# Splitting each attention layer's last unit into two head pairs, with a PSUM bank reserved for the first pair's prologue

## The chip, the cores and the metric

The kernel runs on one core of a Trainium2 chip. The metric is the device time of one execution, in microseconds (us). "Clock" is the mean granted clock of TensorE, as a share of full speed, as the profile's windows give it. PE is TensorE, ACT is ScalarE, DVE is VectorE, POOL is GpSimd. All times are of fast runs, unless a run is called slow.

## The reference, cut to what matters

```python
def _A_ref(x, wq, wk, wv, wo):            # S = 2048, D = 512, 32 heads of 16, one k and one v for all heads
    q = ((x @ wq).reshape(B, S, H, Dh)).transpose(0, 2, 1, 3)
    k = x @ wk;  v = x @ wv
    scores = einsum("bhqd,bkd->bhqk", q, k) * (Dh ** -0.5)
    o = einsum("bhqk,bkd->bhqd", softmax(scores), v)
    return o.transpose(0, 2, 1, 3).reshape(B, S, H * Dh) @ wo
def _B_ref(x, w_gate, w_up, w_down):      # hidden size 1792
    return (gelu(x @ w_gate) * (x @ w_up)) @ w_down
x = A_x                                   # then the same two blocks, twice
x = x + _A_ref(_layernorm(x), ...);  x = x + _B_ref(_layernorm(x), ...)
x = x + _A_ref(_layernorm(x), ...);  x = x + _B_ref(_layernorm(x), ...)
```

## The kernel before

Each attention layer is cut into 32 units of 512 queries and four heads. A unit goes through two passes and a step between them:

- Pass 1 computes scores with the queries on the partitions, and DVE takes the row maxima: 32 pairs of score matmuls, 32 reductions.
- The prologue turns the maxima into extra rows of the query operand, so that the second pass's matmul subtracts them by itself: a combine on DVE, three small POOL steps, four PE transposes into a PSUM bank, a copy by ACT (named AUGS in the profile), and two small DMAs.
- Pass 2 computes the scores again, with the keys on the partitions: 64 matmuls, 64 exponentials on ACT, and 16 groups of four matmuls with V ("PV"), which use four column tiles of the PE array.

The kernel has a static list scheduler of its own. The program is written unit by unit: the query projection of unit u+2, pass 1 and prologue of unit u, the epilogue (normalization, and at times the output projection) of unit u-1, pass 2 of unit u. So pass 1 of a unit runs beside pass 2 of the unit before. PSUM banks 0 to 3 belong to pass 1, bank 7 to PV, and banks 4 to 6 are handed round by `take_c` to everything else. Who waits for a bank is fixed by the order in which the program takes it.

```python
C_B = [4, 5, 6]
PV_B = 7
def take_c():
    b = C_B[cnt["nC"] % 3]
    cnt["nC"] += 1
    return b

def pass1_and_prologue(u):
    for pair in range(NBLK // 2):                       # 32
        ...
        mm = P.add("pe", ... matmul(PS[:, b, :], lhsT=QA[...], rhs=KA[a][...]) ...)      # mm1, L728
        rd = P.add("dve", ... tensor_reduce(out=PM[...], in_=PS[:, b0:b0 + 2, :], ...))  # L734
    cmb = P.add("dve", ...)                             # combine, L746
    hi = P.add("pool", ...); ng = P.add("pool", ...); lo = P.add("pool", ...)
    M_B = take_c()
    ...                                                 # 4 transposes into M_B, L768
    aev = P.add("act", ... out=AUGS[0:8, slot, :], in_=PSB[M_B][0:8, 0:512] ...)         # L771
    for k in range(2):
        dmas.append(P.add("sp", ... dma_start(QA[16 + k:16 + k + 97:32, ...], AUGS[...]) ...))   # L777

def pass2(u):
    for kb in range(NKB):                               # 16 key blocks
        for jj in range(4):
            ...
            b = take_c()
            deps = banks.deps(b)
            if kb == 0 and jj == 0:
                deps = deps + dmas                      # the unit's first score waits for the prologue
            mm = P.add("pe", ... matmul(PS[:, b, :], lhsT=KA[a][...], rhs=QA[...]) ...)  # mm2, L799
            ex = P.add("act", ... activation(out=PT[:, buf, :], in_=PS[:, b, :], func=ACTF.Exp, scale=SCALE) ...)  # L810
            banks.release(b, [ex])
        for j in range(4):
            pv = P.add("pe", ... matmul(PS[32 * j:32 * j + 32, PV_B, :], lhsT=VA[:, kb, :], rhs=PT[:, buf, :],
                       tile_position=(0, 32 * j)), ..., grp=(4 if j == 0 else 1), ...)   # L824

for u in range(NU + 1):
    if u < NU:
        if u + QAHEAD < NU:
            q_proj(u + QAHEAD)
        pass1_and_prologue(u)
    if u >= 1:
        epilogue(u - 1)
    if u < NU:
        pass2(u)
```

`grp` is the number of matmuls that the scheduler keeps together on PE. The rest of this text calls the pass 2 of a layer's last unit, unit 31, the layer's tail.

## Time and profile before

The kernel took 2896.9 us, the median of four runs (2896.36 to 2900.84).

| What (profile of before) | Value |
|---|---|
| Share of the chain that ended last: row maxima on DVE / exponentials on ACT | 58% / 17% |
| A steady unit: 32 reductions | 36.5 us |
| 64 exponentials beside them | 31.46 us |
| Tail of layer 1: 64 exponentials | 37.76 us (1249.50 to 1287.26) |
| Last exponential of unit 30 to first of unit 31 | 4.97 us |
| Granted clock in the tail | 0.50 |

The first lines are of the profile page of before: the busy times, the clock in tenths over 40 slices of the span, the chain that ended last by line, and the two costliest groups (line, engine, operation, destination and source, count, then busy time, mean ns of one, idle time before them and what ended most of it).

```profile
PE 2553.5 (88%) x15853; PEld 925.4 (32%) x15968; DVE 2545.3 (88%) x2650; ACT 2336.6 (81%) x4720; POOL 167.0 (6%) x375
...
PEclk8799999999999999969969999999999999999699
...
DVE PM L734 58%; ACT SH L810 17%; PE PS L970 3%; PE PS L963 3%; PE PS L992 3%; PE PS L799 3%; PE PS L728 1%; PE PS L824 1%; ACT XNT L583 1%; PE PS L904 1%; PE PS L665 1%; PE PS L574 1%; DMA QA<-AUGS 1%; ACT ONT L892 1%; PE PS L621 0%
...
L734 DVE TENSOR_REDUCE PM<-PS 128x2 f32<-128x1024 f32 x2048 | 2329.4, 1211 | 22.4 <-PE PS L728 15.3
L810 ACT ACTIVATE SH<-PS 128x512 bf16<-128x512 f32 x4096 | 2019.5, 692 | 114.2 <-PE PS L799 114.1
```

DVE's row maxima bound the steady units, and the change takes none of them away. What it can alter is where the tail has no partner. The clock line dips to 6 tenths in three of the 40 slices; the 18th (1231 to 1303 us) and the 38th (2678 to 2751 us) hold the two tails.

The next lines are of the timeline of ACT around the first layer's end, in before. Columns: start us, us, engine, line, operation, count, and in brackets the idle time before it and what ended it.

```profile
1213.07 31.46 ACT L810 ACTIVATE SH<-PS 128x512 bf16<-128x512 f32 x64 [2.12 <-PE PS L799]
...
1246.21 0.57 ACT L771 ACTIVATE AUGS<-PS 8x512 bf16<-8x512 bf16 x1
...
1249.50 3.53 ACT L810 ACTIVATE SH<-PS 128x512 bf16<-128x512 f32 x7 [2.24 <-PE PS L799]
1253.34 2.06 ACT L810 ACTIVATE SH<-PS 128x512 bf16<-128x512 f32 x4 [0.31 <-PE PS L799]
...
1286.66 0.60 ACT L810 ACTIVATE SH<-PS 128x512 bf16<-128x512 f32 x1 [0.32 <-PE PS L799]
1287.28 1.28 ACT L976 ACT_TABLE_LOAD   x1
```

Unit 30's 64 exponentials run without a break. Then ACT waits for the prologue of unit 31, and from 1253 on it stops 0.32 us after every four exponentials: ACT is no longer what limits the tail, PE is. The windows of before show why. Columns: window, its length, busy us and instructions of PE, PE's weight loads, DVE, ACT and POOL, then the clock, the DMA share and GB/s.

```profile
1243.82:1247.24 3.42, 2.75 (x28) 1.98 (x28) 2.57 (x7) 3.33 (x7) 0.97 (x3) 1.00 0.00 0
1247.24:1250.65 3.41, 1.20 (x7) 0.24 (x5) 0.63 (x3) 1.17 (x4) 1.57 (x3) 1.00 0.01 2
1250.65:1254.06 3.41, 3.15 (x11) 0.67 (x11) 0.00 (x0) 3.10 (x7) 0.00 (x0) 0.50 0.00 0
1256.00:1264.00 8.00, 6.95 (x26) 1.35 (x25) 0.00 (x0) 7.05 (x15) 0.00 (x0) 0.50 0.00 0
```

At half clock a score matmul takes 0.60 us and a PV group 0.62 us, and the chain of four exponentials is 2.38 us, against 1.97 us for four exponentials at ACT's own pace. One turn of this chain, from before's PE timeline:

```profile
1261.14 0.60 PE L799 MATMUL PS<-QA,KA 64*128 64x512 bf16 x1 [0.26 <-ACT SH L810]
1261.67 0.62 PE L824 MATMUL PS<-SH,VA 128*32 128x512 bf16 x4
1262.22 1.03 PE L799 MATMUL PS<-QA,KA 64*128 64x512 bf16 x3
```

### The profile page before, as it was taken

To read this page: it belongs to the slowest core of one execution; us is meant where nothing else is said; L and a number is where in the kernel's file an instruction comes from. 1 tells how busy PE (TensorE), PEld (TensorE's weight loads), DVE (VectorE), ACT (ScalarE), POOL (GpSimd) and SP (SyncE) were. 2 spreads that over 40 slices of the span, in tenths; PEclk is the share of its full clock that TensorE was granted. 3 is DMA by queue.
4 is the path that set the end of the run, shared out by engine and by line. 5 is a ranking of instruction groups with operands and counts; after the bars stand their busy time and mean duration, and the time that the engine had idled before them with its cause. 6 is when DMAs were issued, how large, how long until landed. Compare 5 with 4: busy or idle time off the path is not lost.

```text
span 2895.3 us, 40074 instructions
## 1 busy us (share of the span) xinstructions
PE 2553.5 (88%) x15853; PEld 925.4 (32%) x15968; DVE 2545.3 (88%) x2650; ACT 2336.6 (81%) x4720; POOL 167.0 (6%) x375
## 2 busy tenths in 40 slices
PE   4899999899999899889968999888999999888898
PEld 1222232222222222227722222222232223222366
DVE  6999999999999999925569999999999999999143
ACT  2699989998999899973418999899989999999632
POOL 3000000001000100010000000100010001000100
PEclk8799999999999999969969999999999999999699
DMA  3000000000000000000000000000000000000000
GB/s 120 1 1 1 1 1 1 1 1 1 1 1 1 1 1 1 1 1 1 1 1 1 1 1 1 1 1 1 1 1 1 1 1 1 1 1 1 1 16 16
DMA packets 10413, 13.88 MB, mean 5 GB/s; under 512 B 1776, under 2 KB 9200, under 8 KB 10224
## 3 DMA queue, kind: packets, MB, share of 16 engines
q1 hardware_dynamic: 10224, 11.31, 1.2%
q8 instruction: 125, 2.05, 0.3%
q14 instruction: 64, 0.52, 0.1%
HBM read 8.68 MB, written 2.10 MB: 4 GB/s over the span
## 4 chain that ended last, share of the span: by engine, by line
DVE 60%; ACT 20%; PE 18%; issue 1%; DMA 1%; POOL 1%; SPq 0%; DVEq 0%; ACTq 0%
DVE PM L734 58%; ACT SH L810 17%; PE PS L970 3%; PE PS L963 3%; PE PS L992 3%; PE PS L799 3%; PE PS L728 1%; PE PS L824 1%; ACT XNT L583 1%; PE PS L904 1%; PE PS L665 1%; PE PS L574 1%; DMA QA<-AUGS 1%; ACT ONT L892 1%; PE PS L621 0%
## 5 line engine op out<-in xcount | busy, mean ns | idle before, releaser
L734 DVE TENSOR_REDUCE PM<-PS 128x2 f32<-128x1024 f32 x2048 | 2329.4, 1211 | 22.4 <-PE PS L728 15.3
L810 ACT ACTIVATE SH<-PS 128x512 bf16<-128x512 f32 x4096 | 2019.5, 692 | 114.2 <-PE PS L799 114.1
L799 PE MATMUL PS<-QA,KA 64*128 64x512 bf16 x4096 | 1470.9, 399 | 119.6 <-ACT SH L810 17.0
L728 PE MATMUL PS<-KA,QA 64*128 64x512 bf16 x4096 | 1003.0, 398 | 125.5 <-DVE PM L734 117.9
L799 PEld LDWEIGHTS PS<-QA,KA 64*128 64x128 bf16 x4096 | 370.6, 94 | 1059.2 <-ACT SH L810 1000.9
L824 PE MATMUL PS<-SH,VA 128*32 128x512 bf16 x4096 | 425.5, 401 | 0.3
L728 PEld LDWEIGHTS PS<-KA,QA 64*128 64x128 bf16 x4096 | 203.8, 94 | 387.3 <-DVE PM L734 306.1
L981 DVE TENSOR_TENSOR HT<-PS,GEL 128x256 bf16<-128x256 f32 x224 | 94.8, 423 | 257.2 <-PE PS L970 166.3
L976 ACT ACTIVATE GEL<-PS 128x256 bf16<-128x256 f32 x224 | 85.9, 384 | 192.1 <-PE PS L963 192.1
L824 PEld LDWEIGHTS PS<-SH,VA 128*32 128x32 bf16 x4096 | 107.6, 93 | 247.4 <-issue 245.8
L970 PE MATMUL PS<-XNT,WU 128*128 128x256 bf16 x896 | 134.5, 273 | 2.3 <-ACT XNT L583 2.3
L963 PE MATMUL PS<-XNT,WG 128*128 128x256 bf16 x896 | 134.4, 273 | 0.0
L754 POOL TENSOR_SCALAR MHL<-MXC 128x16 bf16<-128x16 f32 x64 | 16.3, 255 | 1962.9 <-DVE MXC L746 1962.9
L992 PE MATMUL PS<-WD,HT 128*128 128x512 bf16 x403 | 123.7, 379 | 5.3 <-DVE HT L981 2.4
L771 ACT ACTIVATE AUGS<-PS 8x512 bf16<-8x512 bf16 x64 | 37.2, 581 | 85.6 <-PE PS L768 84.8
L963 PEld LDWEIGHTS PS<-XNT,WG 128*128 128x128 bf16 x896 | 86.9, 98 | 51.9 <-ACT RT L911 0.6
L970 PEld LDWEIGHTS PS<-XNT,WU 128*128 128x128 bf16 x896 | 86.9, 98 | 14.8 <-ACT XNT L583 4.8
L672 ACT ACTIVATE QA<-PS 128x512 bf16<-128x512 f32 x60 | 35.8, 597 | 44.1 <-PE PS L665 44.1
L665 PE MATMUL PS<-XNT,WQP 128*128 128x512 bf16 x196 | 55.5, 400 | 10.6 <-ACT SH L810 8.2
L574 PE MATMUL PS<-IDENT_B,XN 128*128 128x128 bf16 x256 | 28.5, 247 | 39.6 <-ACT XNT L583 20.6
L583 ACT ACTIVATE XNT<-PS 128x512 bf16<-128x512 bf16 x64 | 37.3, 595 | 30.2 <-PE PS L574 30.0
L869 POOL TENSOR_TENSOR SH<-OT,RI 128x256 bf16<-128x256 f32 x64 | 39.7, 620 | 362.0 <-DVE RI L862 357.3
(67 smaller groups left out, 673.7 us busy)
## 6 DMA issues: line engine op xcount, KB each, us to landing
SH<-in_A_x_dram SPq DMA_DIRECT2D x4, 512.0 KB
QA<-AUGS SPq DMA_DIRECT2D x128, 4.0 KB
out_dram<-SH SPq DMA_DIRECT2D x4, 512.0 KB, 2.9
WG<-in_B_w_gate_dram SPq DMA_DIRECT2D x1, 1792.0 KB
WU<-in_B_w_up_dram SPq DMA_DIRECT2D x1, 1792.0 KB
WD<-in_B_w_down_dram SPq DMA_DIRECT2D x1, 1792.0 KB
ONT<-in_A_wq_dram SPq DMA_DIRECT2D x1, 512.0 KB
WO<-in_A_wo_dram SPq DMA_DIRECT2D x1, 512.0 KB
```

What stands on the lines that cost most here:

```text
L583: ev = P.add("act", lambda e, tb=tb, b=b: e.activation(out=XNT[:, :, tb * 128:(tb + 1) * 128], in_=PSB[b][:, 0:NCC * 128].rearrange("p (c ...
L665: mm = P.add("pe", lambda e, cc=cc, qc=qc, g=g, b=b: e.matmul(PS[:, b, :], lhsT=WQP[:, cc, g, :], rhs=XNT[:, cc, qc * 512:(qc + 1) * 512], ...
L728: mm = P.add("pe", lambda e, b=b, tt=tt, a=a, g=g, qc=qc, qb=qb, kc=kc: e.matmul(PS[:, b, :], lhsT=QA[64 * tt:64 * tt + 64, g, (4 * qc + q ...
L734: rd = P.add("dve", lambda e, b0=b0, slot=slot, c0=c0: e.tensor_reduce(out=PM[:, slot, c0:c0 + 2 * NKC + 1:2 * NKC], in_=PS[:, b0:b0 + 2, ...
L799: mm = P.add("pe", lambda e, b=b, tt=tt, a=a, g=g, qc=qc, kb=kb: e.matmul(PS[:, b, :], lhsT=KA[a][64 * tt:64 * tt + 64, kb * 128:(kb + 1) ...
L810: ex = P.add("act", lambda e, b=b, buf=buf: e.activation(out=PT[:, buf, :], in_=PS[:, b, :], func=ACTF.Exp, scale=SCALE), [mm] + bdeps + x ...
L824: pv = P.add("pe", lambda e, j=j, kb=kb, buf=bufs[j]: e.matmul(PS[32 * j:32 * j + 32, PV_B, :], lhsT=VA[:, kb, :], rhs=PT[:, buf, :], star ...
L963: mg = P.add("pe", lambda e, cc=cc, fc=fc, t0=t0, G_B=G_B: e.matmul(PS[:, G_B, 0:256], lhsT=WG[:, cc, fc * 128:(fc + 1) * 128], rhs=XNT[:, ...
L970: mu = P.add("pe", lambda e, cc=cc, fc=fc, t0=t0, U_B=U_B: e.matmul(PS[:, U_B, 0:256], lhsT=WU[:, cc, fc * 128:(fc + 1) * 128], rhs=XNT[:, ...
L976: ga = P.add("act", lambda e, gs=gs, G_B=G_B: e.activation(out=GEL[:, gs, 0:256], in_=PS[:, G_B, 0:256], func=ACTF.Gelu_apprx_tanh), [mg] ...
L981: hm = P.add("dve", lambda e, gs=gs, hs=hs, U_B=U_B: e.tensor_tensor(out=HT[:, hs, 0:256], in0=PS[:, U_B, 0:256], in1=GEL[:, gs, 0:256], o ...
L992: dmm[qb] = P.add("pe", lambda e, pfc=pfc, phs=phs, qb=qb: e.matmul(PS[:, D_B[qb], 0:D], lhsT=HT[:, phs, qb * 128:(qb + 1) * 128], rhs=WD[ ...
```

## The change

The intent is to hide the last unit's prologue. The last unit of each layer becomes two half units, head pair 0 and head pair 1. Each half has its own query copy (QAX, so the prologue's DMA into one half does not touch the other), 16 reductions, 32 exponentials, and PV groups of two. The first half's prologue can then run while unit 30's exponentials are still going, and the second half's while the first half's are. A prologue there needs a PSUM bank in the middle of a pass 2 that was written before it, so the bank is reserved at that point of pass 2 (after 30 of unit 30's 64 scores; after 26 of the first half's 32), and later users of it wait for the prologue's copy.

```diff
+    def reserve(self, b):
+        res = dict(bank=b, before=list(self.rel[b]), waiters=[], done=False)
+        self.rel[b] = []
+        self.pending[b] = res
+        return res
+    def note_user(self, b, op): ...          # the next user of a reserved bank is put on its waiters
+    def fulfill(self, res, release_op):      # ... and waits for the prologue's copy
+        for w in res["waiters"]:
+            w.deps.append(release_op)
 ...
+        QAX = sb("QAX", [128, max(1, 2 * NSPLIT), 512], BF16)      # NSPLIT = 1
 ...
+            for u in range(NU):
+                if u >= NU - NSPLIT:
+                    subs.append((u, [0], False))
+                    subs.append((u, [1], True))
+                else:
+                    subs.append((u, [0, 1], True))
 ...
-                M_B = take_c()
+                res = st.get("reserved")
+                if res is not None:
+                    M_B = res["bank"]
+                    bdeps = res["before"]
+                else:
+                    M_B = take_c()
 ...
-            def pass2(u):
+            def pass2(si, reserve_at=None):
 ...
+                            if reserve_at is not None and nblk == reserve_at:
+                                st["reserved"] = banks.reserve(take_c())
 ...
-                            deps, est=214, q=Q_PV, lane=("col", j), grp=(4 if j == 0 else 1), name="pv", banks=[PV_B])
+                            deps, est=214, q=Q_PV, lane=("col", j), grp=(nh if idx == 0 else 1), name="pv", banks=[PV_B])
 ...
+                        nb = 2 * len(subs[si][1]) * NKB
+                        r_at = max(0, nb // 2 - 2) if len(subs[si][1]) == 2 else max(0, nb - 6)
+                    pass2(si, reserve_at=r_at)
```

## The prediction

> **What bounds the kernel now.** The chain of waits gives 58% of the span to DVE's row-maximum reductions (2048, about 1.13 us apart), 17% to ACT's exponentials. In each of two attention layers 32 units are pipelined: unit u's 32 reductions (36.5 us on DVE) run beside unit u-1's 64 exponentials (31.46 us, 0.49 each). There DVE is full, and the change alters no work. What it can alter is each layer's end, where the last unit's exponentials have no partner. Timeline of layer 1: last reduction ends 1244.15; the prologue (combine, three POOL steps, transposes, copy, DMA) until the first exponential at 1249.50; exponentials until 1287.26: 37.8 us for 64, not 31.46. Layer 2 is the same.
>
> **Why this tail is slow.** In the windows table the granted clock is 1.00 up to 1250.65, then 0.50 until 1298.4. In slices of 3.41 us (the grid of this trace's clock changes), the one before the fall (1247.24 to 1250.65) has PE busy only 1.20 us: PE waits 1.6 us for the prologue's DMA. [...] At half clock the tail's chain is score matmul 0.60, PV 0.55, score matmul 0.59, exponential 0.59 = 2.38 us per four exponentials, against 1.97 at ACT's own rate.
>
> **What the change does.** The last unit becomes two halves (16 reductions, 32 exponentials each). The first half's prologue runs amid unit 30's exponentials, in a bank reserved there; the second's amid the first half's exponentials (after 26 of 32, by the built order). It adds one ACT copy (0.6 us, in ACT's slack), a second small prologue, and twice as many PV groups, of two. It does not overlap more reductions with exponentials: all 32 still run beside unit 30. The gain is only
>
> 1. the 5.0 us between unit 30's last exponential (1244.5) and the next (1249.5), of which four ACT evacuations (2 us) plus about 0.8 us of waits remain: -2.2 us;
> 2. no DMA wait on PE, so I expect the clock to stay at 1.00 and the tail to run at ACT's rate: 31.5 instead of 37.8 us: -6.3 us;
> 3. costs: AUGS copy and reserved bank's stall in unit 30's exponentials, +1.0 to +1.5 us; second AUGS copy +0.5 us.
>
> Net about -6.5 us per layer, all on the critical path: -13 us. The epilogue after the tail (13 us) has its own PE gaps; I give it no gain.
>
> **Predicted: 2884 us, 8-in-10 range 2873 to 2896.** Faster by over 2%: 0.01; within 2%: 0.98; slower by over 2%: 0.01.
>
> **What would show it.** Timeline of ACT: no gap over 1 us between the last reduction and the following exponentials; last exponential some 36 us after unit 30's last, not 42.7; gaps of 0.32 us per four exponentials gone. Windows: clock 1.00 through most of the tail. Score matmul in the tail 0.39, not 0.60 us. Around unit 30's 32nd exponential one ACT gap near 1 us with the AUGS copy. Steady units unchanged.
>
> **What would make it wrong.** If a lull at the handover still drops the clock, PV groups of two alternate with score pairs at half clock (about 1.2 us per two exponentials, or worse) and step 2 is lost: 2890 to 2900. If the reserved bank stalls PE long enough to starve DVE, step 3 grows. If the epilogue also keeps full clock, 3 us more per layer.

Its sum is -2.2 - 6.3 + 1.5 to + 2.0 us, about -6.5 us per layer and -13 us in all. That the clock would stay at 1.00 (step 2) was the estimate from before's windows (PE busy for 1.20 of 3.41 us before the fall).

## The result, and the profile after

The changed kernel took 2885.6 us (median of 9 runs, 2883.59 to 2895.17); before took 2896.56 us in the same rounds (13 runs, 2894.91 to 2902.26). The ratio is 0.9964, with a 95% interval of 0.9955 to 0.9974: within 2%. Ratios here are the mean time of one kernel's fast runs over that of the other's fast runs of the same rounds, so not quite the ratio of the medians quoted. 0.9964 of 2896.9 us is a gain of 10.4 us.

The same lines of the page of after (line 793 is the reductions, 906 the exponentials, 894 the second pass's scores, 920 PV):

```profile
PE 2552.2 (89%) x15861; PEld 928.0 (32%) x15976; DVE 2546.4 (88%) x2652; ACT 2335.2 (81%) x4724; POOL 167.8 (6%) x382
...
PEclk8799999999999999999968999999999999999999
```

The work is the same within a few us on every engine; what differs is the clock: the dips of the 18th and the 38th slice are gone. The timeline of ACT around the first layer's end, in after:

```profile
1210.57 3.72 ACT L906 ACTIVATE SH<-PS 128x512 bf16<-128x512 f32 x7 [2.12 <-PE PS L894]
...
1227.37 0.57 ACT L851 ACTIVATE AUGS<-PS 8x512 bf16<-8x512 bf16 x1
1228.42 15.79 ACT L906 ACTIVATE SH<-PS 128x512 bf16<-128x512 f32 x32 [0.48 <-PE PS L894]
...
1249.25 11.87 ACT L906 ACTIVATE SH<-PS 128x512 bf16<-128x512 f32 x24 [1.77 <-PE PS L894]
1260.82 0.59 ACT L851 ACTIVATE AUGS<-PS 8x512 bf16<-8x512 bf16 x1
1261.31 2.96 ACT L906 ACTIVATE SH<-PS 128x512 bf16<-128x512 f32 x6
1264.48 15.79 ACT L906 ACTIVATE SH<-PS 128x512 bf16<-128x512 f32 x32 [0.22 <-PE PS L894]
1280.29 1.28 ACT L1078 ACT_TABLE_LOAD   x1
```

The first half's AUGS copy now stands in the middle of unit 30's exponentials, where it and the wait for the reserved bank cost 1.05 us (0.57 + 0.48). The second stands in the first half's exponentials and costs 0.5 us. After 1249.25 the exponentials run at ACT's pace, 0.49 us each, in runs of 24 and 32 without the stops of 0.32 us. The windows of after (same columns as above):

```profile
1240.00:1244.00 4.00, 3.58 (x23) 1.10 (x21) 3.31 (x5) 4.00 (x9) 0.65 (x3) 1.00 0.00 0
1244.00:1248.00 4.00, 3.61 (x20) 1.78 (x20) 2.48 (x7) 3.25 (x7) 0.22 (x1) 0.63 0.00 0
1256.00:1264.00 8.00, 7.69 (x35) 2.29 (x35) 0.00 (x0) 8.00 (x18) 0.00 (x0) 1.00 0.01 2
```

In layer 1 the clock falls at the handover and comes back within one window of 3.41 us. In layer 2 it does not fall there at all. In both layers it also falls for two windows at the start of unit 30 (1210.90 to 1217.73 us in layer 1), where before's clock stayed at 1.00.

The following table is worked out from the timelines of ACT, for both layers; it is the yardstick for the experiments too. "Last two units" is from the first exponential of unit 30 to the end of the last of unit 31. "Epilogue" is from there until the FFN's steady stream of GELUs begins. At ACT's pace, the exponentials of "last two units" would take 2 x 31.46 = 62.9 us; the rest is waiting, copies, and PE at half clock.

| Kernel (profiled run) | Last two units, layer 1 / 2 | Epilogue, layer 1 / 2 |
|---|---|---|
| before | 74.19 / 74.19 | 13.54 / 13.48 |
| after | 69.70 / 68.19 | 14.20 / 13.07 |

The gain in these segments is 4.49 + 6.00 - 0.66 + 0.41 = 10.2 us, which is the gain that the runs show. The two profiled runs differ by more (2895.3 and 2882.5 us); 2.5 us of that are in layer 1 before unit 30, where the programs do the same, in units whose clock varies from run to run. The steady units are alike: from one unit's first reduction to the next unit's it is most often 36.55 or 37.02 us, some 40 where the query chunk changes, and on average 37.2 us in both kernels.

Where in "last two units" did it come from? In layer 1 of before: unit 30 31.46, the wait 4.97, the tail 37.76. In after, unit 30 took 33.64 us and the rest 36.06 us. In layer 2 of after these were 33.64 and 34.55 us.

### The profile page after: what moved, and what is told of

Same layout as the page of the kernel before. It is cut to its first block, busy times and chain, and to the rows that moved or that the text cites. A ratio compares the mean times of both kernels' runs of the same rounds, so it can differ in the third digit from the quotient of the medians.

```text
span 2882.5 us, 40111 instructions
## 1 busy us (share of the span) xinstructions
PE 2552.2 (89%) x15861; PEld 928.0 (32%) x15976; DVE 2546.4 (88%) x2652; ACT 2335.2 (81%) x4724; POOL 167.8 (6%) x382
## 4 chain that ended last, share of the span: by engine, by line
DVE 64%; ACT 18%; PE 16%; issue 1%; DMA 0%; POOL 0%; SPq 0%; DVEq 0%; ACTq 0%
DVE PM L793 63%; ACT SH L906 15%; PE PS L1072 3%; PE PS L1065 3%; PE PS L1094 3%; PE PS L894 2%; PE PS L787 1%; ACT XNT L609 1%; PE PS L1000 1%; PE PS L600 1%; ACT ONT L988 1%; PE PS L920 1%; PE PS L691 1%; DVE MXC L817 0%; PE PS L647 0%
## 5 line engine op out<-in xcount | busy, mean ns | idle before, releaser
L894 PE MATMUL PS<-QA,KA 64*128 64x512 bf16 x3968 | 1416.4, 393 | 107.4 <-ACT SH L906 8.3
L787 PE MATMUL PS<-KA,QA 64*128 64x512 bf16 x3968 | 971.1, 397 | 119.1 <-DVE PM L793 110.9
L894 PEld LDWEIGHTS PS<-QA,KA 64*128 64x128 bf16 x3968 | 360.4, 93 | 1008.0 <-ACT SH L906 955.7
L920 PE MATMUL PS<-SH,VA 128*32 128x512 bf16 x4096 | 432.8, 395 | 0.6
L787 PEld LDWEIGHTS PS<-KA,QA 64*128 64x128 bf16 x3968 | 197.8, 94 | 376.5 <-DVE PM L793 296.4
L827 POOL TENSOR_SCALAR MHL<-MXC 128x16 bf16<-128x16 f32 (+1 forms) x66 | 16.8, 255 | 1959.4 <-DVE MXC L817 1896.0
L600 PE MATMUL PS<-IDENT_B,XN 128*128 128x128 bf16 x256 | 28.7, 248 | 37.8 <-ACT XNT L609 20.0
```

The lines of the kernel that those rows point to most:

```text
L787: mm = P.add("pe", lambda e, b=b, tt=tt, a=a, qb=qb, kc=kc, si=si: e.matmul(PS[:, b, :], lhsT=qa_tile(si, tt)[:, qb * 128:(qb + 1) * 128], ...
L894: mm = P.add("pe", lambda e, b=b, tt=tt, a=a, kb=kb, si=si: e.matmul(PS[:, b, :], lhsT=KA[a][64 * tt:64 * tt + 64, kb * 128:(kb + 1) * 128 ...
L920: pv = P.add("pe", lambda e, j=j, kb=kb, buf=bufs[j]: e.matmul(PS[32 * j:32 * j + 32, PV_B, :], lhsT=VA[:, kb, :], rhs=PT[:, buf, :], star ...
```

## The experiments

Twelve runs were made, all with correct outputs; two of them (0 and 11) repeat a kernel. The theory of the prediction (H1) is: before's tail is slow because PE waits for the prologue's DMA, the lull drops the clock, and the change removes the lull. Rivals: (H2) the tail itself is too light for PE to hold the clock, and what helps is that PV groups of two make PE work longer; (H3) the gain is the prologue hidden behind exponentials, and the clock is a side effect.

### 0. The change again

The same kernel as after, as a control on the chip of experiments 1 to 3.

> The changed kernel again, as a control on the chip of this batch. Every theory: 0.9964 of the time before, some 10 us less, with 1 us or 2 of scatter. If the clock is what sets the tail, runs with a lower mean granted clock are the longer ones (0.001 of clock is about 0.8 us in the ten runs that came with the result).

Measured: 2888.72 us (2886.85 to 2896.25), before on that chip 2900.68 us; ratio 0.9963 (0.9948 to 0.9978). The result repeats. The profiled run was the slowest of the four, with a mean clock of 0.917, where the others had 0.961 to 0.963: the granted clock read 0.95 wherever other runs show 1.00. In it the clock fell for one window at the handover in both layers, and the last two units took 69.67 and 69.31 us; in the profile of after it fell in layer 1 alone. From its windows:

```profile
1256.00:1264.00 8.00, 7.94 (x37) 2.45 (x36) 0.00 (x0) 8.00 (x18) 0.00 (x0) 0.95 0.00 0
```

### 1. The split without the reserved bank

```diff
-                    pass2(si, reserve_at=r_at)
+                    pass2(si, reserve_at=None)
```

The half units and their groups of two stay; the prologues are no longer given a bank amid the exponentials.

> Split kept, reservation taken out: each half unit's prologue waits for the exponentials before it, so the first prologue's 5.0 us gap comes back and a second gap of about 4 us appears between the halves. Clock theory: the clock falls to 0.50 after each gap but comes back within one or two 3.4 us windows, because PV groups of two keep PE busier; from unit 30's first exponential to the last one 74 to 77 us (74.2 before, 69.7 and 68.2 after), time 2893 to 2902 us. Rival (the gain is the hidden prologue alone, the clock is incidental): the tail's pace stays 2.38 us per four, 78 us or more, time 2904 us or more.

Measured: 2896.16 us, ratio 0.9984 (0.9969 to 0.9999); last two units 73.83 and 73.34 us. Most of the gain is gone. The split alone does little, and the second half's prologue shows what a hole does. From its windows:

```profile
1262.00:1266.00 4.00, 3.70 (x19) 1.15 (x17) 0.00 (x0) 3.65 (x8) 0.00 (x0) 1.00 0.00 0
1266.00:1268.00 2.00, 0.00 (x0) 0.00 (x0) 0.00 (x0) 0.00 (x0) 0.00 (x0) 1.00 0.02 6
1270.00:1278.00 8.00, 8.00 (x27) 1.66 (x26) 0.00 (x0) 7.29 (x15) 0.00 (x0) 0.50 0.00 0
```

The first half ran at full clock: there the wait after unit 30 was short (0.72 us on ACT), with other copies of ACT and other matmuls of PE before it. Before the second half ACT stood idle for 3.07 us (2.58 us in layer 2), PE did nothing from 1266 to 1268 (2696 to 2698 in layer 2), the clock fell, and the second half stayed at 0.50 to its end although PE was busy throughout. The time is as expected; that the clock would fall at the first half too, and come back within one or two windows, was a miss.

### 2. Before, with the wait filled

Before's PE waits 1.63 us for the prologue's DMA. Here 16 of the FFN's gate and up matmuls, which follow in the program, are repeated there, so that PE has work; their results are overwritten by the real ones.

```diff
+                        NF = 2 if (hc == 0 and fc == 0) else 0
+                        for r in range(NF):
+                            for w, W, B in ((0, WG, G_B), (1, WU, U_B)):
+                                for cc in range(NCC):
+                                    deps = ([evs[-1], ld_wg, ld_wu] + banks.deps(B)) if cc == 0 else []
+                                    P.add("pe", ... matmul(PS[:, B, 0:256], lhsT=W[:, cc, ...], rhs=XNT[:, cc, ...], ...), ..., name="fill")
```

> The kernel before, unsplit, with 16 repeated FFN matmuls (1.7 us at full clock, same results written twice more) in PE's wait for the last prologue's DMA. Clock theory: granted clock stays 1.00 through the tail, exponentials at 0.49 us each, tail 31.5 to 32.5 us instead of 37.8, time 10 to 13 us less than before, as much as the change brought, with nothing hidden. Rival (hidden prologue): no gain, within 2 us of before. [...]

Measured: 2900.5 us, ratio 0.9997 (0.9981 to 1.0014); last two units 74.49 and 73.82 us. No gain. The filler did its part: PE was busy through the wait. Yet the clock fell once the exponentials had started. From its windows:

```profile
1246.00:1250.00 4.00, 3.74 (x31) 2.77 (x31) 1.84 (x6) 1.70 (x4) 1.57 (x3) 1.00 0.01 2
1250.00:1251.00 1.00, 0.69 (x2) 0.19 (x2) 0.00 (x0) 1.00 (x3) 0.00 (x0) 1.00 0.00 0
1251.00:1252.00 1.00, 0.79 (x4) 0.19 (x3) 0.00 (x0) 1.00 (x4) 0.00 (x0) 0.99 0.00 0
1252.00:1253.00 1.00, 1.00 (x7) 0.31 (x6) 0.00 (x0) 1.00 (x3) 0.00 (x0) 0.50 0.00 0
```

This speaks against H1: the fall comes without the DMA wait. In the last two us before the fall the tail with groups of four kept PE busy for only 0.7 to 0.8 of the time. In layer 2 it was the same, 4.1 us after the exponentials began.

### 3. Before, with PV in groups of two in the last unit

```diff
+                    PAIRS = (u == NU - 1)
+                    for i, j in enumerate((0, 2, 1, 3) if PAIRS else (0, 1, 2, 3)):
 ...
-                            ... grp=(4 if j == 0 else 1), name="pv", banks=[PV_B])
+                            ... grp=((2 if i % 2 == 0 else 1) if PAIRS else (4 if i == 0 else 1)), name="pv", banks=[PV_B])
```

The order (0, 2, 1, 3) puts the two heads that are scored together into one PV group. The number of matmuls is the same; the number of groups doubles.

> The kernel before, unsplit, prologue and its gap untouched; only the last unit's PV groups are of two instead of four, as the split makes them. Clock theory with recovery: the clock falls to 0.50 after the gap and comes back within one or two windows of 3.4 us; tail 33 to 35 us instead of 37.8, time 6 to 10 us less than before. Rivals: if only the missing lull matters the clock stays at 0.50 and the tail at 37 to 39 us, time as before; if the hidden prologue is all, the same.

Measured: 2891.77 us (2891.54 to 2893.3), ratio 0.997 (0.9955 to 0.9985); last two units 73.26 and 71.55 us. The clock fell after the wait, as in before, but it came back: after some 30 us in layer 1 (1250.3 to 1281) and some 20 us in layer 2 (2680.5 to 2701). The expectation of one or two windows was far too short. From its windows, at half clock:

```profile
1246.00:1250.00 4.00, 1.90 (x15) 1.03 (x13) 1.57 (x5) 1.76 (x5) 1.57 (x3) 1.00 0.01 2
1274.00:1278.00 4.00, 4.00 (x14) 0.82 (x13) 0.00 (x0) 3.77 (x8) 0.00 (x0) 0.50 0.00 0
```

PE is busy for all of the 4 us and the clock stays at 0.50. Of the gain of some 9 us only 0.93 + 2.64 = 3.6 us are in these segments. They are compared with a profile of before from another chip, and the rest is not explained; below is what runs scatter by.

A PV group costs PE the same, of four or of two. At half clock it took 0.62 us in before, and in this kernel's PE timeline:

```profile
1274.63 0.61 PE L825 MATMUL PS<-SH,VA 128*32 128x512 bf16 x2
1275.18 0.60 PE L799 MATMUL PS<-QA,KA 64*128 64x512 bf16 x2
1275.71 0.61 PE L825 MATMUL PS<-SH,VA 128*32 128x512 bf16 x2
```

At full clock it is 0.40 us of four and 0.39 us of two (after's PE timeline, 1242.62 and 1256.59 us). So two groups of two keep PE busy for about twice as long as one of four, for the same arithmetic.

### 4 and 11. The wait filled, and every second score matmul issued twice

If H2 is right, any other work that keeps PE busy should do as well. This is experiment 2, and in the last unit each score matmul with `tt == 0` is issued twice, while PV stays in groups of four.

```diff
+                        if u == NU - 1 and tt == 0:
+                            P.add("pe", ... the same matmul into the same bank ..., grp=2, name="mm2dup", banks=[b])
```

> Unsplit, filler in the last prologue's wait as in the second experiment, PV groups of four, and in the last unit every second score matmul issued twice (same result): 0.43 us more PE work at full clock per four exponentials, as much as groups of two add. Work theory ([...] groups of two matter because they run PE longer): clock 1.00 through the tail, exponentials at 0.49 us, tail 31.5 to 33 us, 10 to 13 us less than the kernel before. Rival (the shape of the groups, or their closer alternation with the scores, is what counts): clock falls as in the second experiment, no gain, or a slower tail at half clock, 0 to 20 us more.

Measured: three fast runs of 2884.3, 2884.82 and 2899.2 us (mean clock 0.966, 0.966 and 0.956), ratio 0.9974 (0.9947 to 1.0001). The profiled run was slow, 3771.94 us, and tells nothing of the tail, so the kernel was run again:

> The fourth experiment again, whose profiled run fell in a slow state (3772 us) and whose timed runs were 2884.3, 2899.2 and 2884.8 us. Work theory: a fast profile shows the clock at 1.00 through both tails and exponentials at 0.49 us, time 2883 to 2886 us where it stays, with some runs that fall to 0.50 and stay there (the doubled scores make the half-clock tail no faster).

Measured: 2889.33 us (2888.94 to 2891.54), ratio 0.9966 (0.9951 to 0.998), and the last two units took 68.17 and 68.15 us, the clock 1.00 through both tails. The tails are as expected; the time is above the expected 2883 to 2886 us, in rounds in which before was 2.5 us longer too (2899.23 us). From the ACT timeline and a window of the second run of this kernel (816 is the exponentials' line there):

```profile
1252.20 31.47 ACT L816 ACTIVATE SH<-PS 128x512 bf16<-128x512 f32 x64 [2.52 <-PE PS L805]
...
1262.00:1266.00 4.00, 3.77 (x21) 1.02 (x20) 0.00 (x0) 4.00 (x10) 0.00 (x0) 1.00 0.02 4
```

Useless work on PE brought the tail to ACT's pace. That is H2, without PV groups of two.

### 5. Before, with the wait filled and PV in groups of two

The edits of experiments 2 and 3 together. There is no split and no reserved bank; the prologue is as exposed as in before.

> Unsplit, filler in the wait and PV groups of two in the last unit. Work theory: neither the wait nor the tail lets the clock fall; tail 31.5 to 32.5 us in both layers, 11 to 13 us less than the kernel before, about the changed kernel's gain with the prologue still exposed. Rival (hidden prologue): no more than the pairs alone brought (9 us), the clock falling in the wait as before.

Measured: 2882.76 us (2882.26 to 2886.44), before in these rounds 2896.7 us; ratio 0.9953 (0.9939 to 0.9968). The last two units took 67.95 and 67.94 us. From its ACT timeline and windows:

```profile
1212.22 31.46 ACT L810 ACTIVATE SH<-PS 128x512 bf16<-128x512 f32 x64 [2.12 <-PE PS L799]
...
1248.70 31.47 ACT L810 ACTIVATE SH<-PS 128x512 bf16<-128x512 f32 x64 [2.30 <-PE PS L799]
...
1246.00:1250.00 4.00, 3.42 (x27) 2.16 (x24) 0.98 (x5) 1.70 (x4) 1.57 (x3) 1.00 0.01 2
1250.00:1254.00 4.00, 4.00 (x17) 1.12 (x16) 0.00 (x0) 4.00 (x10) 0.00 (x0) 1.00 0.00 0
1274.00:1278.00 4.00, 4.00 (x19) 1.20 (x17) 0.00 (x0) 4.00 (x10) 0.00 (x0) 1.00 0.01 2
```

This is the experiment that decides. Against experiment 2 only the PV grouping differs: 0.50 becomes 1.00. Against experiment 3 only the filler differs: a tail that needed 20 or 30 us to recover never fell. And without the split, the last two units are as fast as with it (67.95 against 69.70 and 68.19): H3 falls as the account of the gain. What the hidden prologue is worth net can be read off the split kernel of experiment 6 below, which has other edits too but a clock of 1.00 all through the last two units: 67.70 and 67.34 us against 67.95, so some 0.25 to 0.6 us per layer.

### 6 and 7. The change, with more work for PE in all units

If the clock is what is worth money, can the whole kernel be kept at 1.00? In experiment 6 the mm1 matmuls of the first eight reductions of each unit are issued twice (and of all of unit 0), and PV goes in pairs in the last six key blocks of unit 30. Experiment 7 also puts 4, 9 and 5 filler matmuls into the waits of the last epilogue and lets the first GELU depend on the copy of the PV bank instead of the last exponential.

```diff
+                            REP = 2 if (si == 0 or (npair < 8 and alist[0] == 0)) else 1
+                            for r, tt in [(r, tt) for r in range(REP) for tt in range(2)]:
 ...
+                    PAIRS = (nh == 4 and u == NU - NSPLIT - 1 and kb >= NKB - 6)
 ...                                               # only in experiment 7:
+                fill(4, unit_pvs[u])
+                fill(9, [])
+                    fill(5, [])
-  ... [mg] + gdeps + ([state["last_exp"]] if (hc == 0 and fc == 0 ...) else [])
+  ... [mg] + gdeps + ([state["last_oev"]] if (hc == 0 and fc == 0 ...) else [])
```

> The changed kernel, with the score matmuls of the first eight reductions of every unit (and all of unit 0) issued twice, and PV groups of two for the last six key blocks of the unit before the last. If short falls of the clock at unit borders cost the steady units their 0.47 us (37.02 where some others take 36.55) and the hand-over 2 to 3 us, this brings 6 to 16 us more than the changed kernel, ratio to before 0.991 to 0.994. If the steady units are bound by DVE whatever the clock, no more than 5 us; if the doubled matmuls get in DVE's way, slower than the changed kernel.

> The same, and in the epilogue after the last unit filler matmuls into a free bank in three waits of PE, and the first GELU (with its 1.28 us table load) placed after the copy of the last unit's output instead of ahead of it. Expected 4.5 us less per layer (1.7 us for the order on ACT, 2.5 to 3 us for the output projection at full clock): 6 to 9 us less than the run before this one, ratio to before near 0.989. If the clock falls all the same, only the 3 us for the order.

Measured: experiment 6 2903.33 us, ratio 1.0026 (1.0011 to 1.0041), mean clock 0.993; experiment 7 2898.65 us, ratio 1.0004 (0.9988 to 1.0021), mean clock 0.995. Both are misses. The clock did hold, and the last two units took 67.70 and 67.34 us, but the steady units got longer: from one unit's first reduction to the next unit's it is 37.51 us on average instead of 37.2. The window of experiment 6 that holds the last two units of layer 2, then the same stretch of 300 us in before, and in experiment 6:

```profile
2654.00:2723.00 69.00, 65.61 (x344) 20.13 (x344) 34.92 (x38) 66.63 (x135) 3.48 (x10) 1.00 0.00 1
```

```profile
600.00:900.00 300.00, 271.50 (x1665) 85.84 (x1673) 297.51 (x283) 276.03 (x557) 16.37 (x38) 0.99 0.00 1
```

```profile
600.00:900.00 300.00, 275.78 (x1774) 85.22 (x1782) 294.52 (x278) 272.71 (x549) 16.86 (x38) 1.00 0.00 1
```

DVE finished 278 instructions where before finished 283. The extra matmuls come ahead of the reductions that bound the steady units, and there was hardly any clock to win there; that they are what held DVE back is the nearest reading, not tested apart. Experiment 7's epilogue was shorter, 11.04 and 11.06 us against 14.20 and 13.07; the run gained 4.7 us on experiment 6, less than the 6 to 9 expected, and the ratio expected near 0.989 was far off.

### 8. Experiment 5 with the epilogue's edits

The edits of experiment 5, and those of experiment 7's epilogue, on before.

> The unsplit kernel with filler and PV groups of two (2882.8 us), and the epilogue's two edits: filler matmuls in three waits of PE, and the first GELU after the copy of the last unit's output. In the run with both on the changed kernel the stretch from the last exponential to the first FFN GELU took 11.0 us instead of 13.0 (this kernel without them). Expected 2 to 3 us less per layer: 2876 to 2879 us, ratio to before 0.993 to 0.994, the fastest of all.

Measured: 2882.86 us (2880.11 to 2885.6, 6 runs), before in these rounds 2899.23 us (11 runs); ratio 0.9942 (0.993 to 0.9955). It has the lowest ratio of all, but the median misses the expectation of 2876 to 2879, and it is not to be told from experiment 5. The clock was 1.00 through all of 1195 to 1310 and 2610 to 2740, and the epilogue took 11.36 us. The 1.6 us that this saved in layer 1 were not to be found later: unit 30 of layer 2 started at 2636.12 us, and at 2635.61 us in experiment 5.

### 9 and 10. The change with PV pairs at the handover

Experiment 9 is after with PV in pairs in the last six key blocks of unit 30, nothing doubled elsewhere. Experiment 10 adds the epilogue's edits.

```diff
+                    PAIRS = (nh == 4 and u == NU - NSPLIT - 1 and kb >= NKB - 6)
+                    ho = (0, 2, 1, 3) if PAIRS else heads
```

> The changed kernel, only with PV groups of two also in the last six key blocks of the unit before the last, so that the clock should not fall at the hand-over. Work theory: the clock stays 1.00 from there to the last exponential, 67.5 to 68 us from unit 30's first exponential to the last one in both layers (69.7 and 68.2 in the changed kernel); 1 to 4 us less than the changed kernel, ratio 0.995 to 0.996. If hiding the prologue were worth its 5 us a layer, this would beat the unsplit kernel with filler and groups of two (0.9953) by 6 us or more, ratio near 0.993; if the split gives it back in its own costs, the two are within 3 us.

> The run before with the epilogue's two edits as well: 4 to 6 us less than it, ratio to before 0.993 to 0.9945, and within 3 us of the unsplit kernel with the same edits.

Measured: experiment 9 2886.5 us, ratio 0.996 (0.9946 to 0.9975), last two units 70.08 and 67.91 us; experiment 10 2883.5 us, ratio 0.9945 (0.9931 to 0.9958), 68.10 and 67.91 us. Experiment 10 gained 3.0 us on experiment 9, not 4 to 6, and is within 1 us of experiment 8, as expected. Experiment 9 is a miss in layer 1: the clock fell there all the same, only later. From its windows:

```profile
1249.00:1253.00 4.00, 3.42 (x16) 0.89 (x14) 0.20 (x2) 3.33 (x7) 1.54 (x3) 1.00 0.00 0
1253.00:1257.00 4.00, 4.00 (x15) 0.92 (x14) 0.00 (x0) 3.75 (x8) 0.00 (x0) 0.53 0.00 0
```

PE was busy for 3.42 of the 4 us before it. In experiment 10, whose source differs only in the last epilogue, it did not fall. So what happens at the handover varies, and these runs do not tell what decides it.

### What the experiments give together

| Kernel | PE in the wait | PV in the tail | Last two units, layer 1 / 2 | Clock in the tail | Ratio |
|---|---|---|---|---|---|
| before | waits 1.63 us | fours | 74.19 / 74.19 | 0.50 | 1 |
| 2 | filled | fours | 74.49 / 73.82 | 0.50 soon | 0.9997 |
| 3 | waits 1.63 us | twos | 73.26 / 71.55 | 0.50 for 20 to 30 us | 0.997 |
| 5 | filled | twos | 67.95 / 67.94 | 1.00 | 0.9953 |
| 11 | filled | fours, scores doubled | 68.17 / 68.15 | 1.00 | 0.9966 |
| 1, split only | idle for over 2 us before the second half | twos | 73.83 / 73.34 | 0.50 in the second half | 0.9984 |
| after | no wait for a DMA | twos | 69.70 / 68.19 | 1.00 but for one fall | 0.9964 |
| 9 | no wait for a DMA | twos | 70.08 / 67.91 | 1.00 but for one fall | 0.996 |

In these runs the clock was 1.00 in the whole tail, but for the one fall of after and of 9, only where two things came together: no wait of PE of 1.63 us or more before or in the tail, and a tail with PV in twos or every second score doubled (PE busy for 4.00 of 4 us in experiment 5 and 3.77 in 11, against 0.69 and 0.79 of the last two us before the fall in experiment 2). The change brings the first by the reserved bank and the second by the way, because half units have PV groups of two.

Runs scatter with the clock. Over 25 runs of before, each thousandth more of the mean clock goes with 1.0 us less; over 13 of after (the profiled run of experiment 0, with its level of 0.95, excluded) it is the same slope. Before's runs have a mean clock of 0.9505 and after's of 0.9615. Drawn on to 0.9615, before's line gives 2888.0 us; after's mean is 2887.2 us. This is an extrapolation, since before never had more than 0.954, but it says the same as the segments: at equal clock the change is worth about 1 us.

## Why the prediction was right, and where its reasons were not

The time was right: 2884.0 us predicted (2873 to 2896), 2885.6 us measured, and "within 2%" had been given 0.98. The gain was put at 13 us, and 10.4 us were measured. That the time was right is in part luck: of the two things that went with a held clock, the prediction saw one and listed the other as a danger, and the split brought both. Point by point:

- "It does not overlap more reductions with exponentials." This held. The steady units and the work of DVE did not change.
- Steps 1 and 3, the exposed prologue (-2.2 us) and the costs (+1.5 to +2.0 us), were put at about -0.5 us per layer together. This was about right where the clock holds: the unsplit kernel of experiment 5 needs 67.95 us for the last two units, the split one of experiment 6 67.70 and 67.34 us. In after itself, with 68.19 us at best, the 5 us of the prologue are all given back, in layer 1 with more: 2.2 us in unit 30 (1.05 us for the AUGS copy and the bank, the rest in a stretch at its start in which the clock was 0.50), 3.9 us in layer 1 and 2.6 us in layer 2 at the handover (four copies by ACT among the first exponentials, and a last wait of 1.77 and 0.97 us), and 0.5 us for the second AUGS copy. "Around unit 30's 32nd exponential one ACT gap near 1 us" was right: 1.05 us.
- Step 2, the size: "the tail to run at ACT's rate: 31.5 instead of 37.8 us: -6.3 us". Where the clock held, this was right: 31.47 us in experiments 5 and 11, and in after 24 and 32 exponentials in 11.87 and 15.79 us. After falls short of it by the one fall at the handover in layer 1.
- Step 2, the reason: "no DMA wait on PE, so I expect the clock to stay at 1.00". This is the step that failed. Experiment 2 took the wait away and the clock fell. It had been read from the window before the fall, 1.20 us busy of 3.41, which is a cause that is enough (experiment 3 falls in it too) but not the only one. The prediction listed the PV groups of two only as a danger, a slower chain at half clock. In these runs they made the difference: with the wait filled, groups of four fell to 0.50 (experiment 2) and groups of two held 1.00 (experiment 5). The half-clock pace itself was right: 2.38 us per four exponentials in experiment 3 as in before (the four terms named for it add to 2.33; before's chain has 0.05 us of issue besides).
- "Clock 1.00 through most of the tail": right in layer 2, and in layer 1 but for 1245 to 1248.5. "Last exponential some 36 us after unit 30's last": 36.06 and 34.55 us. "Score matmul in the tail 0.39": right. "No gap over 1 us" on ACT at the handover: right in layer 2 (0.97 us), wrong in layer 1 (1.77 us).
- "The epilogue ... I give it no gain": right, 14.20 and 13.07 us against 13.54 and 13.48.

What the traces show of the clock: in before and after it has two levels, 0.50 and 1.00 (0.95 in place of 1.00 in experiment 0), and the times between its changes (53 in before's trace, 57 in after's) are all whole multiples of 3.41 us. Before's clock fell to 0.50 at 1250.65 and rose at 1298.4, 47.75 us or 14.0 windows later. The length of PE's wait does not by itself tell when the clock falls: it was at least 2.00 us in experiment 1 in both layers, 1.63 us in before and experiment 3, and in experiment 2 no gap was over 0.47 us, and each of them lost the clock; experiment 5 had a gap of 0.47 us at the same place and kept it.

What stays open is what decides the clock. It is not PE's busy time as the profile gives it: 4.00 of 4.00 us did not raise the clock in experiment 3 for 20 to 30 us, while 3.42 of 4.00 preceded a fall in experiment 9. In before each fall came after a window of 3.41 us in which PE was busy for at most 2.21 us, but other windows of 2.02 us and more kept 1.00, and the fall at after's handover came after one of 3.00 us; so no threshold of busy time comes out of these traces.

## What to carry to other kernels

When a phase of a kernel has little work for PE and yet depends on PE's speed, look at the granted clock in that phase before counting the waits: here the 10 us came with the held clock, and hiding the prologue was worth at most 0.6 us a layer net. Test the two apart with filler on PE, since a wait that stands just before a fall need not be its only cause; experiment 5, two small edits to the old kernel, did at least as well as the whole change (ratio 0.9953 against 0.9964, the intervals overlap). Two cheap ways to give PE more work in the tail held its clock at 1.00 here: PV in groups of two, each of which takes PE as long as a group of four (0.39 and 0.40 us at full clock), and every second score matmul issued twice (with the wait filled, 67.95 and 68.17 us for the last two units, against 74.49 with the wait filled alone). More work for PE in every unit did not pay: 37.51 us from unit to unit instead of 37.2, ratio 1.0026 (experiment 6).

## What the traces leave open

- How much work of PE brings the clock back. In experiment 3 PE was busy for all of eight windows of 3.41 us in a row in layer 1, and of six in layer 2, before the clock came back.
- What makes it fall where PE does not wait long. In experiment 2 it fell after PE had been busy for 0.69 and 0.79 us of the last two us, with no gap over 0.47 us.
- Where the level of 0.95 that the profiled run of experiment 0 showed in place of 1.00 comes from.
- What the cause is of a slow run like that of experiment 4: 3771.94 us, with score matmuls of 629 ns on average against 399 ns in before. That is near the 0.60 us of before's half-clock tail, although the clock on record is 1.00 (at 2000 to 2010 us), so in that run the recorded clock does not account for the pace. From its groups:

```profile
L805 PE MATMUL PS<-QA,KA 64*128 64x512 bf16 x4096 | 1910.0, 629 | 4.8 <-ACT SH L816 3.5 <-DMA QA<-AUGS 0.9
```
